# Decode with grouped attention and a gated feed-forward: the feed-forward's first two weight matrices are loaded at the start of the kernel instead of behind the last head's keys

## The chip, the cores and the metric

The kernel runs on one core of one Trainium2 chip. The metric is the device time of one execution in microseconds (us). The kernel before took 698.38 us, the median of three runs (697.04 to 698.63). Profiles, and all times of single instructions below, come from one profiled execution.

## The reference

One token `x` of width D = 512 goes through two branches, which a scalar gate mixes. All data are float32. Branch A is attention with 32 query heads over 8 key/value heads, 32768 cached positions and head size 128; the keys and values of one head are 16.8 MB each, 268 MB for all heads. Branch B is a SwiGLU feed-forward with F = 1792.

```python
g = sigmoid((x * gate_w).sum(-1))
q = (x @ wq).reshape(32, 128)                    # wq 512 x 4096
p = softmax(q . k_cache / sqrt(128))             # 4 query heads share a key head
a = (p . v_cache).reshape(4096) @ wo             # wo 4096 x 512
b = (silu(x @ w1) * (x @ w3)) @ w2               # w1, w3 512 x 1792, w2 1792 x 512
out = g * a + (1 - g) * b
```

## The kernel before, in words

**Three regions.** SBUF holds three tiles of 64 KB per partition, `ra`, `rb` and `rc` (L56). Each takes half of one head's keys or values, 8.39 MB. In the steady state `ra` holds the first half of a head's keys, `rb` the second half, and `rc` the first and then the second half of the values. So the values have only one region: the second half can't be loaded before the first is used up, nor the next head's first half before this head's second is.

**The load stream.** SP issues every large load (L112 to L146), each behind semaphore waits that say its region is free. At the start these are `wq` into `rc`, then the keys of head 0 into `ra` (two halves, L113 and L114) and `rb` (L115). Then, for each head h: the next head's first keys into `ra` once `scores(0)` of head h has read it (L120); the head's first values into `rc` once `values` of the previous head has read the second ones (L129, a wait for count 2h of `c_v`); the next head's second keys into `rb` once `scores(1)` has read it (L132); the second values into `rc` once the first are read (L134). For the last head there are no next keys. In their place L123 and L124 load `w1` and `w3` into `ra`, 3.67 MB each; the last second values go into `rb` (L136). Then `wo` goes into `ra`, behind a wait until the feed-forward's first products have read it (L138 to L140), and `w2` in four pieces into `rc` (L146).

```python
sp.wait_ge(c_v.sem, 2 * h)                                   # L126
sp.dma_start(rc, vd[h, 0]).then_inc(l_c, 16)                 # L129
sp.wait_ge(c_k.sem, 2 * h + 2)                               # L130
```

**The engines.** VectorE transposes each half of the keys in place in blocks of 32 x 32, eight instructions per half (`turned`, L290 to L295). TensorE's loop over heads (L273) has one body for all heads, with parts under an `If` that head 0 skips. Per head it does `scores(0)` on `ra`; the sum of the exponentials and `values(0)` of the previous head; `scores(1)` on `rb`; `values(1)` of the previous head; `flips`, which brings the scores of all positions of a query head together; `heads`; and `maxima`. VectorE then takes the maximum of the scores, and ScalarE computes the exponentials (L342) that the next iteration's `values` use. So the values of head h are used one iteration after its keys.

**The ends.** Ahead of the loop TensorE computes the gate's sum and the queries (L176, L182), and VectorE lays the queries out (L194, L198). Behind the loop come the gate and up rows of the feed-forward (`ff_rows`, L349 to L361: 16 products of 128 x 448 for each of `w1` and `w3`, two matmul records each), the sigmoid (L364), two multiplications (L366, L369) and a transpose into `htp` (L371); then the last head's `values`, and the products with `wo` and `w2` (L404 to L432). `htp`, `hid` and `omask` are cut out of the tile `sbuf` (L73 to L75), which the loop uses for the scores.

`take` (L105) is TensorE's wait for a token, which it counts down again. `c_k`, `c_v` and `c_e` are counts that `scores`, `values` and the products outside the loop raise when they end.

Of the kernel before, what the change touches and what calls it, by code (L numbers as in the profile page):

```python
# [4 lines left out]
AF = mybir.ActivationFunctionType  # L5
ALU = mybir.AluOpType
# [3 lines left out]
P = 128  # L10
# [14 lines left out]
@with_exitstack  # L25
def kernel(ctx, tc, x, k_cache, v_cache, wq, wo, w1, w3, w2, gate_w, out):
    with tc.tile_critical():
        _program(tc.nc, x, k_cache, v_cache, wq, wo, w1, w3, w2, gate_w, out)


def _program(nc, x, k_cache, v_cache, wq, wo, w1, w3, w2, gate_w, out):
    pe, dve, act, pool, sp = nc.tensor, nc.vector, nc.scalar, nc.gpsimd, nc.sync
    _, HKV, S, DH = k_cache.shape
    D = x.shape[-1]
    F = w1.shape[1]
    HQ = wq.shape[1] // DH
    REP = HQ // HKV
    NC = D // P
    FR = F // P
    FJ = F // 4  # L40
# [5 lines left out]
    def sb(name, *shape):  # L46
        return nc.alloc_sbuf_tensor(name, [P, *shape], F32).ap()

    def token(name):
        return nc.alloc_semaphore(name)  # L50

    def count(name):
        return Count(nc, name)


    ra, rb, rc = sb("ra", W), sb("rb", W), sb("rc", W)  # L56

    ident, ones, fold, dmask = sb("ident", P), sb("ones", P), sb("fold", 32), sb("dmask", 4)
    xs, gw, xp = sb("xs", NC), sb("gw", NC), sb("xp", NC, 32)
# [4 lines left out]
    ob = sb("ob", 512)  # L64
# [3 lines left out]
    gpr, gsm, gate = sb("gpr", NC), sb("gsm", 1), sb("gate", 2)  # L68
# [1 line left out]
    mr = nc.alloc_sbuf_tensor("mr", [REP, 1], F32).ap()  # L70
    md = nc.alloc_sbuf_tensor("md", [REP, REP], F32).ap()
    flat = sbuf.rearrange("p a i m -> p (a i m)")
    htp = flat[:, 0:FR * 32].rearrange("p (k i) -> p k i", i=32)  # L73
    hid = flat[:, 448:448 + FJ]
    omask = flat[:, 896:896 + P]  # L75

    qt = rc[:, 0:1024].rearrange("p (b q c i) -> p b q c i", b=2, q=4, c=4)

# [2 lines left out]
    def bank(n, w=1):  # L81
        return psum[:, 512 * n:512 * (n + w)]

    s_ps = [bank(0), bank(1)]
# [6 lines left out]
    l_w1, l_w3, l_v = token("l_w1"), token("l_w3"), token("l_v")  # L91
# [4 lines left out]
    c_q, c_k, c_v, c_f, c_m, c_n, c_h, c_e = (  # L96
        count(n) for n in ("c_q", "c_k", "c_v", "c_f", "c_m", "c_n", "c_h", "c_e")
    )
    c_dve, c_act, c_pool = count("c_dve"), count("c_act"), count("c_pool")

    t_x, t_tr, t_win, t_ev, t_ob, t_mx, t_md, t_p, t_e = (
        token(n) for n in ("t_x", "t_tr", "t_win", "t_ev", "t_ob", "t_mx", "t_md", "t_p", "t_e")
    )

    def take(sem, n=1):  # L105
        pe.wait_ge(sem, n).then_inc(sem, -n)  # L106
# [3 lines left out]
    vd = v_cache.rearrange("a h (r p n) d -> (a h) r p (n d)", r=2, p=P, n=NK)  # L110
    half = W // 2
    sp.dma_start(rc, wq.rearrange("(p c) n -> p (c n)", c=NC)).then_inc(l_q, 16)  # L112
    sp.dma_start(ra[:, 0:half], kd[0, 0][:, 0:half]).then_inc(l_k0, 16)  # L113
    l_a.by(sp.dma_start(ra[:, half:W], kd[0, 0][:, half:W]), 16)  # L114
    l_b.by(sp.dma_start(rb, kd[0, 1]), 16)  # L115
    for h in range(HKV):

        if h < HKV - 1:
            sp.wait_ge(c_k.sem, 2 * h + 1)
            l_a.by(sp.dma_start(ra, kd[h + 1, 0]), 16)  # L120
        else:
            sp.wait_ge(c_k.sem, 2 * h + 1)
            sp.dma_start(ra[:, 0:NC * F], w1.rearrange("(p c) f -> p (c f)", c=NC)).then_inc(l_w1, 16)  # L123
            sp.dma_start(ra[:, NC * F:2 * NC * F], w3.rearrange("(p c) f -> p (c f)", c=NC)).then_inc(l_w3, 16)  # L124
        if h:
            sp.wait_ge(c_v.sem, 2 * h)  # L126
        else:
            sp.wait_ge(c_dve.sem, 1)
        sp.dma_start(rc, vd[h, 0]).then_inc(l_c, 16)  # L129
        sp.wait_ge(c_k.sem, 2 * h + 2)  # L130
        if h < HKV - 1:
            l_b.by(sp.dma_start(rb, kd[h + 1, 1]), 16)  # L132
            sp.wait_ge(c_v.sem, 2 * h + 1)
            sp.dma_start(rc, vd[h, 1]).then_inc(l_c, 16)  # L134
        else:
            sp.dma_start(rb, vd[h, 1]).then_inc(l_v, 16)  # L136
    wod = wo.rearrange("(p k) e -> p (k e)", k=32)
    sp.wait_ge(c_e.sem, 2)  # L138
    for i in range(2):
        sp.dma_start(ra[:, i * half:(i + 1) * half], wod[:, i * half:(i + 1) * half]).then_inc(l_wo[i], 16)  # L140
    w2t = rc[:, 0:FR * D].rearrange("p (k e) -> p k e", e=D)
# [10 lines left out]
    local = count("local")  # L152
# [25 lines left out]
    for c in range(NC):  # L178
        for b in range(2):
            for j in range(4):  # L180
                o = (c * HKV + 4 * b + j) * REP * DH
                m = pe.matmul(  # L182
                    pq[b][32 * j:32 * j + 32, :], xp[:, c, :], rc[:, o:o + REP * DH],
                    start=(c == 0), stop=(c == NC - 1),
# [11 lines left out]
    for r in range(4):  # L196
        for j in range(4):
# [2 lines left out]
                qt[32 * j:32 * j + 32, :, :, :, 0].rearrange("p b q c -> p b c q"),  # L200
            )
    c_dve.by(m)


    for h in range(HKV):
# [12 lines left out]
    def scores(m, region):  # L218
        for f in range(2):
            for c in range(4):  # L220
                take(t_tr)
                for g in range(4):
                    n = 64 * f + 16 * g
                    w = 16 + 32 * c if f == 0 else 32 * c
                    i = pe.matmul(  # L225
                        s_ps[m][32 * g:32 * g + 32, :], winbuf[:, w:w + 32],
                        region.rearrange("p (n c i) -> p c n i", c=4, i=32)[:, c, n:n + 16],
                        start=(f == 0 and c == 0), stop=(f == 1 and c == 3),
                    )
        i.then_inc(c_k.sem, 1)  # L230

    def values(r, region):
        for g in range(4):
            for f in range(2):
                for t in range(4):
                    w = 512 * r + 64 * (2 * g + f) + 16 * t
                    n = 64 * f + 16 * g + 4 * t
                    i = pe.matmul(  # L238
                        o_ps[32 * t:32 * t + 32, :], prob[:, w:w + 32], region[:, n * DH:(n + 4) * DH],
                        start=(r == 0 and g == 0 and f == 0), stop=(r == 1 and g == 3 and f == 1),  # L240
                    )
        i.then_inc(c_v.sem, 1)

    def flips():
        take(t_ev, 2)
        for a in range(16):
            for s in range(2):
                i = pe.matmul(  # L248
                    pf[64 * s:64 * s + 64, 64 * a:64 * a + 64], sbuf[:, a].rearrange("p i m -> p (i m)"),
                    ident.rearrange("p (gf r s q) -> p s r gf q", gf=8, r=2, s=2)[:, s],  # L250
                    start=True, stop=True,
                )
        i.then_inc(c_f.sem, 1)

    def heads():
        take(t_ob)
        for b in range(4):
            i = pe.matmul(  # L258
                mb[:, 0:REP], ob[:, b * P:(b + 1) * P], fold[:, 4 * b:4 * b + 4], start=(b == 0), stop=(b == 3)
            )  # L260
        i.then_inc(c_h.sem, 1)

    def maxima():
        take(t_mx)
        pe.transpose(ma[0:REP, 0:P], mx, ident).then_inc(c_m.sem, 1)
        take(t_md)
        pe.matmul(ma[:, 128:128 + REP], ones[0:REP, :], md, start=True, stop=True).then_inc(c_m.sem, 1)

    def norm():
        take(t_p, REP)  # L270
        pe.matmul(mc[:, 0:REP], ones, sums, start=True, stop=True).then_inc(c_n.sem, 1)

    with nc.Fori(0, HKV, 1, engines=[PE]) as step:  # L273
        take(t_win, 4)
        scores(0, ra)
        with pe.If(step > 0):
            norm()
            take(l_c, 16)
            values(0, rc)
        scores(1, rb)  # L280
        with pe.If(step > 0):
            take(l_c, 16)
            values(1, rc)
        flips()
        with pe.If(step > 0):
            heads()
        maxima()
# [58 lines left out]
            ).then_inc(t_p, 1)  # L346


    def ff_rows(ps, base):  # L349
        for c in range(NC):  # L350
            for j in range(4):
                o = base + c * F + FJ * j
                i = pe.matmul(
                    ps[32 * j:32 * j + 32, 0:FJ], xp[:, c, :], ra[:, o:o + FJ], start=(c == 0), stop=(c == NC - 1)
                )
        i.then_inc(c_e.sem, 1)

    pe.wait_ge(l_w1, 16)
    ff_rows(s_ps[0], 0)
    pe.wait_ge(l_w3, 16)  # L360
    ff_rows(s_ps[1], NC * F)  # L361
    n_ff = 2
    act.wait_ge(c_e.sem, 1)
    n_sg = c_act.by(act.activation(ob[:, 0:FJ], s_ps[0][:, 0:FJ], AF.Sigmoid))  # L364
    dve.wait_ge(c_act.sem, n_sg)
    n_hid = local.by(dve.tensor_mul(hid, ob[:, 0:FJ], s_ps[0][:, 0:FJ]))  # L366
    dve.wait_ge(c_e.sem, 2)
    dve.wait_ge(local.sem, local.n)
    local.by(dve.scalar_tensor_tensor(hid, s_ps[1][:, 0:FJ], gate[:, 1:2], hid, op0=ALU.mult, op1=ALU.mult))  # L369
    dve.wait_ge(local.sem, local.n)  # L370
    dve.transpose(htp, hid.rearrange("p (a k) -> p k a", k=FR)).then_inc(t_e, 1)  # L371


    norm()
    pe.wait_ge(l_c, 16)
    values(0, rc)
    n_inv = inverted(HKV - 1)
    pe.wait_ge(l_v, 16)
    values(1, rb)
    act.wait_ge(local.sem, n_hid)  # L380
    act.wait_ge(c_v.sem, 2 * HKV)
    act.copy(ob, o_ps).then_inc(t_ob, 1)
    heads()
# [5 lines left out]
        otall.unsqueeze(2).to_broadcast([P, HQ, 4]),  # L389
        dmask.unsqueeze(1).to_broadcast([P, HQ, 4]),  # L390
    ).then_inc(t_e, 1)
    take(t_e, 2)
    pe.matmul(ma[:, 0:32], omask, fold, start=True, stop=True).then_inc(c_e.sem, 1)
    dve.wait_ge(c_e.sem, n_ff + 1)
    dve.tensor_copy(oq[:, 0:32], ma[:, 0:32]).then_inc(t_e, 1)
# [13 lines left out]
    for k in range(W2[1]):  # L409
        t = k % 4  # L410
        i = pe.matmul(  # L411
            acc[32 * t:32 * t + 32, :], htp[:, k, :], w2t[:, k, :], start=False, stop=(k >= W2[1] - 4),
            skip_group_check=True,
        )
# [52 lines left out]
```

## Time and profile before

| | |
|---|---|
| median of 3 runs | 698.38 us |
| profiled execution | 698.76 us |
| its span, first to last instruction | 696.7 us |
| moved from HBM | 296.23 MB, 425 GB/s over the span |
| busy TensorE / VectorE / ScalarE | 54% / 44% / 6% of the span |
| mean granted TensorE clock | 0.784 |

The rows that the sections below quote are of these kinds. A row of the timeline has the start in us from the span's start, the duration in us of one instruction or of a merged run of like ones, the engine and line, the operation, what it writes and reads, the count, and in brackets how long the engine had been idle and what ended that. `SPq` is SP's queue: the row of a load stands at its issue. A row of the list of DMA issues ends with the us from issue to landing, so that issue and this number give the landing. PE is TensorE, DVE VectorE, ACT ScalarE. "issue" as the cause of idle time means that nothing in the profile explains it.

### The profile page before, as it was taken

The numbers are of one execution on the slowest core, as the hardware profiler recorded it, in microseconds if no ns is written. First come the engines' busy times: TensorE is split into PE (matmuls) and PEld (weight loads), VectorE is DVE, ScalarE is ACT, GpSimd is POOL, SyncE is SP. The second block draws the span as 40 slices with busy tenths as digits, with TensorE's granted clock in tenths as the row PEclk, the third lists the DMA queues.
The fourth block names the chain that finished last, engine by engine and source line by source line (L and its number), as shares of the span: only waits on it lengthen the run. The fifth ranks groups of instructions, "written<-read, shape, count | busy, mean of one in ns | idle before, by whom it ended". The sixth has DMA issues, their size and how long they took to land. (4 is left out here: it accounts for less than half of the span.)

```text
span 696.7 us, 6587 instructions
## 1 busy us (share of the span) xinstructions
PE 374.5 (54%) x2944; PEld 104.0 (15%) x2944; DVE 307.9 (44%) x208; ACT 38.7 (6%) x94; POOL 7.1 (1%) x41
## 2 busy tenths in 40 slices
PE   0544457684727363664637472664638371781575
PEld 0100021030101210030101210030103110130122
DVE  0097573916345370917254470918163561810000
ACT  0000110001000100020000100020000100020000
POOL 0000000000000000000000000000000000000000
PEclk9987769787969787686859787687869686696689
DMA  9999998999999999999999999999999999999996
GB/s 399 412 453 411 430 419 369 421 425 467 433 421 421 421 478 425 421 421 433 463 429 421 421 433 463 429 421 421 433 463 429 422 421 433 426 459 426 425 419 276
DMA packets 6353, 296.35 MB, mean 425 GB/s; under 512 B 964, under 2 KB 968, under 8 KB 1224
## 3 DMA queue, kind: packets, MB, share of 16 engines
q1 hardware_dynamic: 6056, 296.23, 98.6%
q8 instruction: 6, 0.10, 0.1%
q10 hardware_dynamic: 288, 0.00, 0.0%
q14 instruction: 3, 0.02, 0.0%
HBM read 296.23 MB, written 0.00 MB: 425 GB/s over the span
## 5 line engine op out<-in xcount | busy, mean ns | idle before, releaser
L295 DVE STREAM_TRANSPOSE rb<-rb 128x2048 f32<-128x2048 f32 x64 | 141.8, 2275 | 141.5 <-DMA rb<-in_A_k_cache_dram 141.5
L225 PE MATMUL psum<-rb,winbuf 128*32 128x512 f32 x512 | 96.7, 835 | 133.6 <-PEq L106 133.5
L295 DVE STREAM_TRANSPOSE ra<-ra 128x2048 f32<-128x2048 f32 x64 | 141.3, 2274 | 39.6 <-DMA ra<-in_A_k_cache_dram 39.6
L225 PE MATMUL psum<-ra,winbuf 128*32 128x512 f32 x512 | 93.0, 801 | 106.0 <-PEq L106 106.0
L238 PE MATMUL psum<-rc,prob 128*32 128x512 f32 x960 | 114.8, 633 | 20.8 <-DMA rc<-in_A_v_cache_dram 16.5
L330 DVE TENSOR_REDUCE mx<-psum 128x4 f32<-128x1024 f32 x8 | 9.8, 1225 | 94.0 <-PE psum L248 94.0
L238 PEld LDWEIGHTS psum<-rc,prob 128*32 128x32 f32 x960 | 34.4, 116 | 96.5 <-issue 79.9
L225 PEld LDWEIGHTS psum<-rb,winbuf 128*32 128x32 f32 x512 | 13.6, 124 | 213.3 <-issue 213.3
L225 PEld LDWEIGHTS psum<-ra,winbuf 128*32 128x32 f32 x512 | 13.5, 122 | 177.3 <-issue 177.0
L310 ACT COPY sbuf<-psum 128x512 f32<-128x512 f32 x16 | 9.9, 620 | 469.0 <-PE psum L225 469.0
L299 DVE SCALAR_TENSOR_TENSOR otall<-psum,gate,recip 128x4 f32<-128x4 f32 x8 | 1.7, 214 | 45.1 <-PE psum L258 45.1
L248 PE MATMUL psum<-ident,sbuf 128*64 128x64 f32 x512 | 18.3, 233 | 5.7 <-issue 4.9
L342 ACT ACTIVATE prob<-psum,nm 128x256 f32<-128x256 f32 x32 | 18.9, 701 | 41.1 <-DVE nm L339 41.1
L248 PEld LDWEIGHTS psum<-ident,sbuf 128*64 128x64 f32 x512 | 17.0, 146 | 13.1 <-issue 13.1
L176 PE MATMUL psum<-gsm,ones 128*128 128x1 f32 x2 | 0.6, 348 | 26.1 <-PEq L106 26.1
L238 PE MATMUL psum<-rb,prob 128*32 128x512 f32 x64 | 8.7, 705 | 9.5 <-DMA rb<-in_A_v_cache_dram 9.5
L212 POOL COPY winbuf<-winraw 32x16 f32<-32x16 f32 x32 | 6.1, 191 | 523.2 <-PE psum L225 484.0
L404 PE MATMUL psum<-ra,oq 128*32 128x512 f32 x64 | 9.0, 711 | 4.2 <-DMA ra<-in_A_wo_dram 3.8
L169 DVE COPY xp<-xs 128x4 f32<-128x4 f32 x1 | 0.2, 171 | 23.2 <-DMA gw<-in_gate_w_dram 23.2
L258 PE MATMUL psum<-fold,ob 128*128 128x4 f32 x64 | 8.4, 255 | 0.9 <-PEq L106 0.9
L182 PE MATMUL psum<-rc,xp 128*32 128x512 f32 x64 | 8.6, 699 | 0.0
L258 PEld LDWEIGHTS psum<-fold,ob 128*128 128x128 f32 x64 | 7.7, 191 | 2.2 <-issue 1.7
(57 smaller groups left out, 71.3 us busy)
## 6 DMA issues: line engine op xcount, KB each, us to landing
ra<-in_A_k_cache_dram SPq DMA_DIRECT2D x2, 4096.0 KB, 36.0
ra<-in_A_wo_dram SPq DMA_DIRECT2D x2, 4096.0 KB, 50.7
ra<-in_B_w_dram SPq DMA_DIRECT2D x2, 3584.0 KB, 43.4
rc<-in_B_w_dram SPq DMA_DIRECT2D x1, 1536.0 KB, 32.7
rc<-in_B_w_dram SPq DMA_DIRECT2D x1, 1024.0 KB, 34.8
rc<-in_B_w_dram SPq DMA_DIRECT2D x1, 768.0 KB, 36.2
rc<-in_B_w_dram SPq DMA_DIRECT2D x1, 256.0 KB, 36.3
rc<-in_A_v_cache_dram SPq DMA_DIRECT2D x15, 31.4
```

What stands on the lines that cost most here:

```text
L182: m = pe.matmul(pq[b][32 * j:32 * j + 32, :], xp[:, c, :], rc[:, o:o + REP * DH], start=(c == 0), stop=(c == NC - 1),)
L212: pool.tensor_copy(winbuf[32 * r:32 * r + 32, 16:144].rearrange("p (c k) -> p c k", k=32)[:, :, 4 * r:4 * r + REP], winraw[32 * r:32 * r + ...
L225: i = pe.matmul(s_ps[m][32 * g:32 * g + 32, :], winbuf[:, w:w + 32], region.rearrange("p (n c i) -> p c n i", c=4, i=32)[:, c, n:n + 16], ...
L238: i = pe.matmul(o_ps[32 * t:32 * t + 32, :], prob[:, w:w + 32], region[:, n * DH:(n + 4) * DH], start=(r == 0 and g == 0 and f == 0), stop ...
L248: i = pe.matmul(pf[64 * s:64 * s + 64, 64 * a:64 * a + 64], sbuf[:, a].rearrange("p i m -> p (i m)"), ident.rearrange("p (gf r s q) -> p s ...
L258: i = pe.matmul(mb[:, 0:REP], ob[:, b * P:(b + 1) * P], fold[:, 4 * b:4 * b + 4], start=(b == 0), stop=(b == 3))
L295: dve.transpose(part[:, c], part[:, c]).then_inc(t_tr, 1)
L299: return local.by(dve.scalar_tensor_tensor(otall[:, REP * h:REP * h + REP], mb[:, 0:REP], gate[:, 0:1], recip, op0=ALU.mult, op1=ALU.mult))
L310: act.copy(sbuf[:, :, :, m], s_ps[m].rearrange("p (n i) -> p n i", i=32)).then_inc(t_ev, 1)
L330: dve.tensor_reduce(mx, pf.rearrange("p (a q) -> p q a", q=REP), axis=AX.X, op=ALU.max).then_inc(t_mx, 1)
L342: act.activation(prob[:, 0:1024].rearrange("p (a n q) -> p n a q", a=16, q=REP)[:, :, :, q], pf.rearrange("p (n a q) -> p n a q", n=16, q= ...
L404: pe.matmul(acc[32 * t:32 * t + 32, :], oq[:, k:k + 32], ra[:, k * D:(k + 1) * D], start=(k < 4), stop=False, skip_group_check=True,)
```

## The change

`w1` and `w3` go into `rb`, right behind `wq` in SP's order and ahead of all keys. The load of head 0's second keys into `rb` then has to wait until both products have read it. The gate and up rows, with all that follows up to `htp`, move from behind the loop to ahead of it. The loads in the last head's place are gone, and so is the wait ahead of `wo`. `htp` must now live through the loop, so it becomes a tile of its own (14 x 32 elements a partition); `hid` and `omask` move inside `sbuf`. TensorE takes the token of the finished `htp` ahead of the loop instead of behind it, and ScalarE's wait for `hid` ahead of its last copy goes.

```diff
-    htp = flat[:, 0:FR * 32].rearrange("p (k i) -> p k i", i=32)
-    hid = flat[:, 448:448 + FJ]
-    omask = flat[:, 896:896 + P]
+    omask = flat[:, 0:P]
+    hid = flat[:, P:P + FJ]
+    htp = sb("htp", FR, 32)
...
     sp.dma_start(rc, wq.rearrange("(p c) n -> p (c n)", c=NC)).then_inc(l_q, 16)
+    sp.dma_start(rb[:, 0:NC * F], w1.rearrange("(p c) f -> p (c f)", c=NC)).then_inc(l_w1, 16)
+    sp.dma_start(rb[:, NC * F:2 * NC * F], w3.rearrange("(p c) f -> p (c f)", c=NC)).then_inc(l_w3, 16)
     sp.dma_start(ra[:, 0:half], kd[0, 0][:, 0:half]).then_inc(l_k0, 16)
     l_a.by(sp.dma_start(ra[:, half:W], kd[0, 0][:, half:W]), 16)
+    sp.wait_ge(c_e.sem, 2)
     l_b.by(sp.dma_start(rb, kd[0, 1]), 16)
     for h in range(HKV):
 
         if h < HKV - 1:
             sp.wait_ge(c_k.sem, 2 * h + 1)
             l_a.by(sp.dma_start(ra, kd[h + 1, 0]), 16)
-        else:
-            sp.wait_ge(c_k.sem, 2 * h + 1)
-            sp.dma_start(ra[:, 0:NC * F], w1.rearrange("(p c) f -> p (c f)", c=NC)).then_inc(l_w1, 16)
-            sp.dma_start(ra[:, NC * F:2 * NC * F], w3.rearrange("(p c) f -> p (c f)", c=NC)).then_inc(l_w3, 16)
...
     wod = wo.rearrange("(p k) e -> p (k e)", k=32)
-    sp.wait_ge(c_e.sem, 2)
...
+    def ff_rows(ps, base):
...
+    pe.wait_ge(l_w1, 16)
+    ff_rows(s_ps[0], 0)
+    pe.wait_ge(l_w3, 16)
+    ff_rows(s_ps[1], NC * F)
...
+    dve.transpose(htp, hid.rearrange("p (a k) -> p k a", k=FR)).then_inc(t_e, 1)
...
+    take(t_e)
     with nc.Fori(0, HKV, 1, engines=[PE]) as step:
...
-    act.wait_ge(local.sem, n_hid)
     act.wait_ge(c_v.sem, 2 * HKV)
...
-    take(t_e, 2)
+    take(t_e)
```

The moved lines are those from L349 to L371, word for word but for `rb` in place of `ra` and `n_hid`, which is no longer kept.

More of the change, by code (lines that the diff above doesn't have):

```diff
@@ L202, in _program @@
     c_dve.by(m)
+    def ff_rows(ps, base):
+        for c in range(NC):
+            for j in range(4):
+                o = base + c * F + FJ * j
+                i = pe.matmul(
+                    ps[32 * j:32 * j + 32, 0:FJ], xp[:, c, :], rb[:, o:o + FJ], start=(c == 0), stop=(c == NC - 1)
+                )
+        i.then_inc(c_e.sem, 1)
+    pe.wait_ge(l_w1, 16)
+    ff_rows(s_ps[0], 0)
+    pe.wait_ge(l_w3, 16)
+    ff_rows(s_ps[1], NC * F)
+    n_ff = 2
+    act.wait_ge(c_e.sem, 1)
+    n_sg = c_act.by(act.activation(ob[:, 0:FJ], s_ps[0][:, 0:FJ], AF.Sigmoid))
+    dve.wait_ge(c_act.sem, n_sg)
+    local.by(dve.tensor_mul(hid, ob[:, 0:FJ], s_ps[0][:, 0:FJ]))
+    dve.wait_ge(c_e.sem, 2)
+    dve.wait_ge(local.sem, local.n)
+    local.by(dve.scalar_tensor_tensor(hid, s_ps[1][:, 0:FJ], gate[:, 1:2], hid, op0=ALU.mult, op1=ALU.mult))
+    dve.wait_ge(local.sem, local.n)
+    dve.transpose(htp, hid.rearrange("p (a k) -> p k a", k=FR)).then_inc(t_e, 1)
     for h in range(HKV):
@@ L346, in _program @@
             ).then_inc(t_p, 1)
[L349 to L371, printed above, removed]
     norm()
```

## The prediction
> **What bounds the kernel now.** I read the page's head first, then the DMA slices and queues, then the chain that ended last, and then the timeline where the change reaches.
>
> ```profile
> PE 374.5 (54%) x2944; PEld 104.0 (15%) x2944; DVE 307.9 (44%) x208; ACT 38.7 (6%) x94; POOL 7.1 (1%) x41
> DMA  9999998999999999999999999999999999999996
> GB/s 399 412 453 411 430 419 369 421 425 467 433 421 421 421 478 425 421 421 433 463 429 421 421 433 463 429 421 421 433 463 429 422 421 433 426 459 426 425 419 276
> q1 hardware_dynamic: 6056, 296.23, 98.6%
> ...
> 680.49 3.77 another core or an unknown queue
> ```
>
> No engine is over 54% busy, while SP's load queue is busy for 98.6% of the span, in every slice but the first heads and the end. Even the end waits for a load: the chain stands still for 3.77 us until the second half of `wo` is there. The kernel is one stream of loads. A change that moves the same bytes is worth only what it adds to or takes from the time in which that queue is **dry**. So the question is where the queue runs dry before and after, and I follow landings (issue plus time to landing).
>
> **The rate and the price of a dry queue.**
>
> ```profile
> 0.95 0.39 SPq L112 DMA_DIRECT2D rc<-in_A_wq_dram  x1
> 2.34 0.71 SPq L115 DMA_DIRECT2D rb<-in_A_k_cache_dram  x1
> 58.69 0.33 SPq L120 DMA_DIRECT2D ra<-in_A_k_cache_dram  x1
> 81.42 0.33 SPq L132 DMA_DIRECT2D rb<-in_A_k_cache_dram  x1
> 121.42 0.33 SPq L134 DMA_DIRECT2D rc<-in_A_v_cache_dram  x1
> ```
>
> Their times to landing, in the same order, from the list of DMA issues:
>
> ```profile
> rc<-in_A_wq_dram SPq DMA_DIRECT2D x1, 22.1
> rb<-in_A_k_cache_dram SPq DMA_DIRECT2D x1, 59.5
> ra<-in_A_k_cache_dram SPq DMA_DIRECT2D x1, 24.6
> rb<-in_A_k_cache_dram SPq DMA_DIRECT2D x1, 40.6
> rc<-in_A_v_cache_dram SPq DMA_DIRECT2D x1, 21.9
> ```
>
> `wq` lands at 23.05 and head 0's second keys at 61.84: 16.78 MB in 38.8 us, 432 GB/s, or 19.4 us for a region of 8.39 MB. Issued into an empty queue, the same bytes need 22.1 (`wq`) or 21.9 us (second values of head 0, issued 0.6 us ahead of the landing, at 122.0, of the keys before them). A dry queue thus costs the time between the landing before and the next issue, plus 21.9 - 19.4 = 2.5 us.
>
> **The end of the stream, where loads are removed.**
>
> ```profile
> 569.81 7.08 PE L238 MATMUL psum<-rc,prob 128*32 128x512 f32 x64
> 576.94 0.33 SPq L134 DMA_DIRECT2D rc<-in_A_v_cache_dram  x1
> 577.31 0.43 SPq L123 DMA_DIRECT2D ra<-in_B_w_dram  x1
> 588.89 8.89 DVE L295 STREAM_TRANSPOSE rb<-rb 128x2048 f32<-128x2048 f32 x4 [21.04 <-DMA rb<-in_A_k_cache_dram]
> 608.44 7.84 PE L238 MATMUL psum<-rc,prob 128*32 128x512 f32 x64
> 616.34 0.33 SPq L129 DMA_DIRECT2D rc<-in_A_v_cache_dram  x1
> 625.29 3.21 PE L353 MATMUL psum<-ra,xp 128*32 128x448 f32 x32 [1.09 <-DMA ra<-in_B_w_dram]
> 628.56 1.63 SPq L140 DMA_DIRECT2D ra<-in_A_wo_dram  x2
> 645.32 9.86 PE L238 MATMUL psum<-rc,prob 128*32 128x512 f32 x64 [16.51 <-DMA rc<-in_A_v_cache_dram]
> 664.68 8.72 PE L238 MATMUL psum<-rb,prob 128*32 128x512 f32 x64 [9.50 <-DMA rb<-in_A_v_cache_dram]
> ```
>
> The loads at 576.94 (the second values of head 6) and at 616.34 (the first of head 7) take, from issue to landing:
>
> ```profile
> rc<-in_A_v_cache_dram SPq DMA_DIRECT2D x1, 31.3
> ...
> rc<-in_A_v_cache_dram SPq DMA_DIRECT2D x1, 28.9
> ```
>
> The first lands at 608.24. The other, the next into `rc`, is issued only at 616.34, since `values(1)` (7.84 us from 608.44) must first have read `rc`, and that stands behind `scores(1)` in TensorE's order, which follows VectorE's eight transposes of the keys that landed at 588.89. Neither can move: the first four transposes alone take 8.89 us, and the other four as long. In between, the queue lives on `w1` and `w3`: they have landed by 625.29, 17.0 us after 608.24 (7.34 MB, 431 GB/s), so the issue at 616.34 comes 9 us before the queue would be empty. That is the cover which the change takes away; in the other heads it is the next head's first keys.
>
> After the change nothing stands in the queue behind the load that lands at 608.24. The first values of head 7, issued at 616.34 on this clock, land 21.9 us later, at 638.24. In the kernel before the landing is at 645.2, so the end comes 7.0 us earlier on this clock, for 17.0 us of bytes taken out. Everything up to there has moved back by the same 7.34 MB at the start, 17.0 us. **Sum: 17.0 - 7.0 = 10.0 us longer**; as a check, 616.34 - 608.24 + 2.5 gives 10.6 less 0.6 for this landing's cadence of 20.0 in place of 19.4. The price has ends: `values` on the rows of this kernel takes from 7.08 (at 569.81) over 7.84 to 9.86 us (at 645.32), so 9.2 to 12.0; I take 10.0, since the row with 7.84 is that very run of instructions.
>
> The rest of the end is neutral. `wo` loses its wait and is issued some 12 us sooner, but it was issued at 628.56, 36 us before the transfer ahead of it landed (664.68): nothing. `w2` still follows `values(0)` and is still queued behind `wo`. The feed-forward's 2 x 3.21 us of TensorE and its ScalarE and VectorE work lay inside the 16.51 us in which TensorE waited for head 7's values: freeing them gives nothing.
>
> **The start, where loads are added.**
>
> ```profile
> 25.54 0.17 DVE L169 COPY xp<-xs 128x4 f32<-128x4 f32 x1 [23.24 <-DMA gw<-in_gate_w_dram]
> 26.59 8.62 PE L182 MATMUL psum<-rc,xp 128*32 128x512 f32 x64
> 36.64 3.10 DVE L198 COPY winraw<-rc 32x32 f32<-32x32 f32 x16
> 39.76 17.66 DVE L295 STREAM_TRANSPOSE ra<-ra 128x2048 f32<-128x2048 f32 x8
> 625.03 0.55 ACT L364 ACTIVATE ob<-psum 128x448 f32<-128x448 f32 x1
> 625.61 0.62 DVE L366 TENSOR_TENSOR sbuf<-ob,psum 128x448 f32<-128x448 f32 x1 [4.35 <-ACT ob L364]
> 628.57 0.69 DVE L369 SCALAR_TENSOR_TENSOR sbuf<-psum,gate,sbuf 128x448 f32<-128x448 f32 x1 [2.34 <-PE psum L353]
> 629.29 0.94 DVE L371 STREAM_TRANSPOSE sbuf<-sbuf 128x448 f32<-128x448 f32 x1
> ```
>
> `wq` still lands at 23.05, `w1` then at 31.5, `w3` at 40.05, the two halves of head 0's first keys at 49.8 and 59.5. TensorE ends the queries at 35.2, does `w1`'s rows by 38.4 and `w3`'s from 40.1 to 43.3. ScalarE's 0.55 us and VectorE's 0.62 (behind its copies, which end at 39.74) lie in the wait for `w3`; then 0.69 + 0.94 end at 45.0, 4.8 us before the first keys land. So VectorE's transposes and TensorE's wait for `htp` don't delay anything; if this cover were gone, there are 10 more us until the second keys land, on which the next step hangs.
>
> **The added wait** is SP's for `c_e` at 2, met at 43.4. Behind it stand the load of head 0's second keys and all later loads. The queue still holds head 0's first keys until 59.5, a cover of 16 us. At nothing: head 0's second keys land at 59.5 + 19.4 = 78.9, which is 61.84 + 17.0. If the small load that holds up `xp` came only with `w1`, 6 us later, the first keys' cover of 4.8 us would be gone to within a microsecond, and the 10 us behind it would still hide that.
>
> **One gain and how it is lost.** Before, head 1's first keys are issued at 58.69, 3 us before the landing at 61.84, because VectorE started only at 39.76; they land at 83.3, 21.5 us after it instead of 19.4. After, VectorE starts at 49.8 and ends at 68.4, and the issue comes some 9 us ahead: up to 2.1 us back. But head 0's second values aren't bound by the stream. Their issue at 121.42 stands 59.6 us behind the landing at 61.84, through transposes, `flips`, maxima, exponentials, transposes and `values(0)`. That chain starts at the same landing and stays: issue at 138.5, landing at 160.4, against 143.3 + 17.0 = 160.3 before. So 0.0. It could only become shorter here:
>
> ```profile
> 82.17 0.65 PE L248 MATMUL psum<-ident,sbuf 128*64 128x64 f32 x14 [0.82 <-PEq L106]
> 87.68 3.04 PE L248 MATMUL psum<-ident,sbuf 128*64 128x64 f32 x50 [4.85 <-issue]
> ```
>
> In the first pass TensorE stops for 4.85 us within `flips`, waiting for nothing that the profile names. In the same 5 us the queue list has one transfer of instructions:
>
> ```profile
> q8 instruction: 1, 0.02, 1.1%
> ```
>
> I read it as a late fetch of code. The change puts 128 matmul and weight-load instructions ahead of this place, so the stop can move. If it goes, the chain loses 4.85 us, of which the stream uses at most 21.3 - 19.4 = 1.9 here plus the 2.1 above: -4.0. If a second one of its size falls into the chain, it costs +4.9. I take 0: the skipped parts of the body are the same.
>
> The Trainium skill, "Runtime: NRT & Kernel Launch", section "Instruction fetch mechanics", says that code is fetched in blocks of 16 KiB (256 instructions), ahead in sequence only, and that a taken branch to a block that isn't there stalls. By that page the stop stays, since head 0 still jumps over `values`, and the estimate would remain 0 with some tenths for the 14 products now behind it; no run here shows that yet.
>
> **Sum.** 698.76 + 10.0 + 0.0 = 708.8 us for an execution like the profiled one (span 696.7 and 2.1 around it). That one lies 0.4 above the median of the runs, so 708.4. The extreme terms, 9.2 - 4.0 and 12.0 + 4.9, seldom fall together.
>
> **The rivals.**
>
> 1. *The stop in `flips` goes* (above): 2 to 4 us less, 704.4 to 706.4. For it: nothing ties the stop to the work. Against it: the parts that head 0 skips ahead of it stay. 0.16.
> 2. *A second hold-up of the size of the stop enters the first head's chain*: 708.4 + 4.9 = 713.3. Against it: the covers of 4.8, 10 and 16 us. 0.08.
> 3. *The stream pays the dry time back*, and the time is the same or less. Place: the 28.8 MB from head 7's values on. Price: it needs 66.8 us at 432 GB/s; to win back 10 us it must run at 508 GB/s, and from there on the change is no loss; at 530 it would end 2.4 us faster, 696.0. For it: slices of up to 478 GB/s in the page's row, though beside slices of 421 to 425. Against it: after the dry queue at 121.42 the landing took 21.9 us, no less than `wq`'s 22.1. 0.03. The Trainium skill, "DMA: Bandwidth & Descriptors", section "Specifications", gives 435 GB/s as the fabric's ceiling; by it this rival can't be, and the 432 measured here lies just below.
>
> That the loads don't land in the new order can't be: they share one queue, and the waits are in the program.
>
> **How the numbers follow.** The forecast has the rest, 0.73. The range of 704.0 to 712.0 goes down to the lower end of `values` with all of rival 1's gain (708.4 - 0.8 - 4.0 = 703.6, a little within it), and up to the upper end of `values` with the 0.7 us of the 14 products (82.17 above) and the runs' own spread of 0.8 on either side (711.9). It leaves out rivals 2 and 3 and a few hundredths of tails, some 0.15. About 0.3% (2.1 us) is what a measurement can tell from no change; every case but rival 3 is beyond it. Rival 3 splits into 0.01 faster and 0.02 within: faster 0.01, same 0.02, slower 0.97.
>
> **What would show it.** In the profile after, the DMA slices have a dip shortly before head 7's first values, and the list of issues gives that load about 21.9 us to landing, not 28.9. Between its landing and the one before lie about 30 us instead of 19.4. SP's wait ahead of `wo` is gone, and the new one, ahead of head 0's second keys, ends near 43 with the queue full. Wrong would be a landing of head 7's first values less than 27 us after the one before, a first key landing delayed by the rows of the feed-forward, or a stream rate other than 432 GB/s for the early `w1` and `w3`.

## The result and the profile after

The changed kernel takes **706.23 us**, the median of 5 runs (705.89 to 707.14), beside 698.38 us for the kernel before (5 runs, 697.04 to 699.98): a ratio of 1.0112 with a 95% interval of 1.0095 to 1.0130, so 7.9 us slower. The forecast was 708.4, the range 704.0 to 712.0. The profiled execution took 706.43 us, with a span of 704.4, 7.7 above the 696.7 of before.

The page's head after, first the DMA slices and what they moved, then SP's load queue:

```profile
DMA  9999999999999999999999999999999999939996
GB/s 410 402 434 422 467 414 428 428 450 424 428 450 428 424 432 450 421 432 440 439 424 424 454 424 432 428 443 432 424 454 424 425 435 443 424 141 466 417 418 273
q1 hardware_dynamic: 6056, 296.23, 97.5%
```

The bytes are the same, 296.23 MB. One slice near the end stands out: the queue is busy 3 tenths and moves 141 GB/s. Before, no slice there was below 9. The stages around it, from the view by windows (the last two columns are the DMA share and GB/s; a packet counts where it starts, so both fall off ahead of a landing):

```profile
603.00:622.00 19.00, 10.70 (x64) 1.62 (x64) 17.73 (x9) 0.00 (x0) 0.00 (x0) 0.78 0.86 373
622.00:632.00 10.00, 9.48 (x134) 4.58 (x131) 0.13 (x1) 1.20 (x2) 0.00 (x0) 1.00 0.32 105
```

The timeline of that place, and then the times to landing of the loads at 591.16 and 629.86:

```profile
591.16 0.33 SPq L133 DMA_DIRECT2D rc<-in_A_v_cache_dram  x1
603.28 8.89 DVE L319 STREAM_TRANSPOSE rb<-rb 128x2048 f32<-128x2048 f32 x4 [21.05 <-DMA rb<-in_A_k_cache_dram]
622.74 7.07 PE L261 MATMUL psum<-rc,prob 128*32 128x512 f32 x64 [0.52 <-PEq L106]
629.86 0.33 SPq L128 DMA_DIRECT2D rc<-in_A_v_cache_dram  x1
652.89 8.54 PE L261 MATMUL psum<-rc,prob 128*32 128x512 f32 x64 [15.01 <-DMA rc<-in_A_v_cache_dram]
672.26 9.09 PE L261 MATMUL psum<-rb,prob 128*32 128x512 f32 x64 [10.84 <-DMA rb<-in_A_v_cache_dram]
...
692.00 3.64 PE L402 MATMUL psum<-ra,oq 128*32 128x512 f32 x32 [3.62 <-DMA ra<-in_A_wo_dram]
```

```profile
rc<-in_A_v_cache_dram SPq DMA_DIRECT2D x1, 31.4
...
rc<-in_A_v_cache_dram SPq DMA_DIRECT2D x1, 23.0
```

Head 6's second values land at 622.56. Nothing is queued behind them. `values` reads them until 629.8, then head 7's first values are issued, and they land at 652.86: 30.30 us behind the landing before, where a full queue has 19.4. This is the dry queue that the prediction worked out, in its place and order. The end still waits for `wo` (3.62 us), as before.

The start:

```profile
41.58 4.84 PE L207 MATMUL psum<-rb,xp 128*32 128x448 f32 x32 [2.80 <-DMA rb<-in_B_w_dram]
46.48 0.33 SPq L118 DMA_DIRECT2D rb<-in_A_k_cache_dram  x1
51.12 8.89 DVE L319 STREAM_TRANSPOSE ra<-ra 128x2048 f32<-128x2048 f32 x4 [2.97 <-DMA ra<-in_A_k_cache_dram]
80.20 17.66 DVE L319 STREAM_TRANSPOSE rb<-rb 128x2048 f32<-128x2048 f32 x8 [10.47 <-DMA rb<-in_A_k_cache_dram]
100.61 2.08 PE L271 MATMUL psum<-ident,sbuf 128*64 128x64 f32 x64 [0.82 <-PEq L106]
133.39 0.33 SPq L133 DMA_DIRECT2D rc<-in_A_v_cache_dram  x1
138.28 8.89 DVE L319 STREAM_TRANSPOSE rb<-rb 128x2048 f32<-128x2048 f32 x4 [15.08 <-DMA rb<-in_A_k_cache_dram]
```

The rows of the feed-forward do what was expected: SP's new wait ends at 46.48 instead of 43.4, still with the queue full until 60.8, and VectorE has done its share when it waits another 2.97 us for head 0's keys. Two things differ that matter. `w3` is there only at 41.57 instead of 40.05. And the first `flips` runs in one piece of 2.08 us: **the stop of 4.85 us is gone**. The records of `flips` are also quicker, 2.08 us for all 64 instead of 0.65 + 3.04, so the chain from the landing of head 0's second keys to the issue of its second values takes 53.2 us instead of 59.6. That issue now comes at 133.39, 4.9 us ahead of the landing of the keys before them instead of 0.6.

Landing by landing, after against before (us; a landing is issue plus time to landing, a distance is the time since the landing before):

| | before | after | shift |
|---|---|---|---|
| head 0's second keys | 61.84 | 80.18 | +18.34 |
| head 1's first keys, distance | 21.45 | 19.31 | -2.14 |
| head 0's second values, distance | 21.30 | 19.34 | -1.96 |
| all other loads up to head 6's second values | | | +0.1 |
| head 6's second to head 7's first values | 37.00 | 30.30 | -6.70 |
| from there to the end of the span | 51.46 | 51.54 | +0.08 |
| sum | | | +7.7 |

### The profile page after: what moved, and what is told of

It reads as the page before. It is cut to its first block, busy times and chain, and to the rows that moved or that the text cites. A ratio compares the mean times of both kernels' runs of the same rounds, so it can differ in the third digit from the quotient of the medians.

```text
span 704.4 us, 6586 instructions
## 1 busy us (share of the span) xinstructions
PE 364.7 (52%) x2944; PEld 101.5 (14%) x2944; DVE 308.1 (44%) x208; ACT 37.4 (5%) x93; POOL 7.1 (1%) x41
## 3 DMA queue, kind: packets, MB, share of 16 engines
q1 hardware_dynamic: 6056, 296.23, 97.5%
HBM read 296.23 MB, written 0.00 MB: 421 GB/s over the span
## 5 line engine op out<-in xcount | busy, mean ns | idle before, releaser
L248 PE MATMUL psum<-rb,winbuf 128*32 128x512 f32 x512 | 91.1, 790 | 148.1 <-PEq L106 148.1
L261 PE MATMUL psum<-rc,prob 128*32 128x512 f32 x960 | 111.4, 617 | 17.1 <-DMA rc<-in_A_v_cache_dram 15.0
L271 PE MATMUL psum<-ident,sbuf 128*64 128x64 f32 x512 | 16.7, 223 | 0.8 <-PEq L106 0.8
L207 PE MATMUL psum<-rb,xp 128*32 128x448 f32 x64 | 8.0, 653 | 2.8 <-DMA rb<-in_B_w_dram 2.8
L402 PE MATMUL psum<-ra,oq 128*32 128x512 f32 x64 | 7.3, 595 | 4.0 <-DMA ra<-in_A_wo_dram 3.6
```

Of the source, the lines that this page charges most:

```text
L207: i = pe.matmul(ps[32 * j:32 * j + 32, 0:FJ], xp[:, c, :], rb[:, o:o + FJ], start=(c == 0), stop=(c == NC - 1))
L248: i = pe.matmul(s_ps[m][32 * g:32 * g + 32, :], winbuf[:, w:w + 32], region.rearrange("p (n c i) -> p c n i", c=4, i=32)[:, c, n:n + 16], ...
L261: i = pe.matmul(o_ps[32 * t:32 * t + 32, :], prob[:, w:w + 32], region[:, n * DH:(n + 4) * DH], start=(r == 0 and g == 0 and f == 0), stop ...
L271: i = pe.matmul(pf[64 * s:64 * s + 64, 64 * a:64 * a + 64], sbuf[:, a].rearrange("p i m -> p (i m)"), ident.rearrange("p (gf r s q) -> p s ...
L402: pe.matmul(acc[32 * t:32 * t + 32, :], oq[:, k:k + 32], ra[:, k * D:(k + 1) * D], start=(k < 4), stop=False, skip_group_check=True,)
```

## The experiments

The theory behind all of them: the load stream is the clock, and the change moves the time only by where the stream runs dry. The rivals: the end is bound by the work behind the last values, or the moved work delays the first head. A second question was why the stop went and what it was.

**1. Head 7's first values into another region.** This takes the wait away by giving it nothing to wait for.

```diff
+            sp.wait_ge(c_k.sem, 2 * h + 1)
+            sp.dma_start(ra, vd[h, 0]).then_inc(l_v0, 16)      # h = 7
...
+    sp.wait_ge(c_v.sem, 2 * HKV - 2)                            # wo now into rc, w2 into ra
+        sp.dma_start(rc[:, i * half:(i + 1) * half], ...).then_inc(l_wo[i], 16)
...
-    values(0, rc)
+    values(0, ra)
```

> The changed kernel, but head 7's first values go into ra (free once scores(0) of head 7 has read the keys), wo into rc and w2 into ra. Theory: the 7.7 us net loss is the load queue running dry ahead of head 7's first values (30.3 us from the landing before to theirs, where a full queue has 19.4). With another region for them their load is issued some 30 us sooner, the landing distance goes to 19.4, and the time falls by 10.9 to about 695.5 us, 2.9 below the kernel before. Rival: the wait is not what costs, the end is held by the products behind the last values, or the stream pays dry time back: then the distance goes to 19.4 as well, but the time stays above 703.

Measured: 695.35 us (6 runs), ratio to the kernel before 0.9959 (0.9945 to 0.9974).

```profile
592.03 0.43 SPq L126 DMA_DIRECT2D ra<-in_A_v_cache_dram  x1
642.31 8.50 PE L266 MATMUL psum<-ra,prob 128*32 128x512 f32 x64 [3.24 <-DMA ra<-in_A_v_cache_dram]
661.66 9.06 PE L266 MATMUL psum<-rb,prob 128*32 128x512 f32 x64 [10.85 <-DMA rb<-in_A_v_cache_dram]
```

The load is issued 31 us ahead of the landing at 622.96 and lands 19.3 us behind it. The span is 693.5, 10.9 below the changed kernel's 704.4: the whole dry time comes back, to a tenth. The theory holds, the rivals fall. This version is faster than both kernels, by 0.4% beside the kernel before.

**2 and 3. The code ahead of the loop made longer.** The same 32 small products, once in the kernel before, once in the changed one.

```diff
+    for b in range(2):
+        for c in range(NC):
+            for j in range(4):
+                pe.matmul(s_ps[b][32 * j:32 * j + 32, 0:P], xp[:, c, :], ones, start=(c == 0), stop=(c == NC - 1))
```

> The kernel before, with 32 small products of xp and ones (128 columns, results never read) put into TensorE's program right behind the queries, as many instructions as the rows of the feed-forward. Nothing else. Theory: the stop of 4.85 us in the first flips is a fetch of code at a block boundary, and only moving the code made it go. Then the first flips runs in one piece (2.1 us instead of 0.65 + 4.85 + 3.04), head 0's second values are issued near 116.5 instead of 121.4 and land 19.4 us behind the keys before them instead of 21.3: about 696.5 us. Rival: the stop belongs to what the loads or the clock do at that moment: it stays, and the time is 698.4.

Measured: 696.85 us (12 runs), ratio 0.9976 (0.9963 to 0.9989). The first `flips`, the issue of head 0's second values, and its time to landing:

```profile
83.35 2.08 PE L254 MATMUL psum<-ident,sbuf 128*64 128x64 f32 x64 [0.82 <-PEq L106]
116.11 0.33 SPq L134 DMA_DIRECT2D rc<-in_A_v_cache_dram  x1
...
rc<-in_A_v_cache_dram SPq DMA_DIRECT2D x1, 25.5
```

Products whose results nobody reads made the kernel before 1.5 us faster. The stop is gone, and the values land at 141.61, 19.3 us behind the keys before them instead of 21.3.

> The changed kernel with the same 32 small products ahead of the loop, so that the code of the loop stands about 256 instructions further on than in the kernel before. Theory of code blocks of 256 instructions: the stop in the first flips is back at nearly the place of the kernel before (after some 12 to 14 of its products), head 0's second values are issued near 138.3 and land about 21.3 us behind the keys before them instead of 19.3: 706.2 + 2.0 = 708.2 us. Rival: the stop came from the loads or from timing: it stays away, 706.2.

Measured: 708.78 us (4 runs), ratio to before 1.0145 (1.0130 to 1.0161), 2.6 us above the changed kernel.

```profile
100.57 0.98 PE L271 MATMUL psum<-ident,sbuf 128*64 128x64 f32 x13 [0.81 <-PEq L106]
104.99 3.04 PE L271 MATMUL psum<-ident,sbuf 128*64 128x64 f32 x51 [3.45 <-issue]
140.27 0.33 SPq L133 DMA_DIRECT2D rc<-in_A_v_cache_dram  x1
```

The stop is back, after 13 records of `flips` where the kernel before had 14. In this execution head 0's second values were issued not near 138.3 but 2.0 us behind the landing of the keys before them, and landed 23.8 us behind it instead of the expected 21.3. It took 710.91, the longest of the four; the other three took 708.6 to 708.9.

**4. The changed kernel without the moved work.** The feed-forward's part of the output is left out.

```diff
-    sp.wait_ge(c_e.sem, 2)
+    sp.wait_ge(l_w1, 16)
+    sp.wait_ge(l_w3, 16)
     l_b.by(sp.dma_start(rb, kd[0, 1]), 16)
...
-    pe.wait_ge(l_w1, 16)
-    ff_rows(s_ps[0], 0)
...
+    dve.memset(htp, 0.0).then_inc(t_e, 1)
```

> The changed kernel without the gate and up rows and what follows from them (htp is set to zero, so the feed-forward's part of the output is left out); w1 and w3 are still loaded, and the load of head 0's second keys waits for their landing alone. Theory: the moved work costs nothing where it stands, so the landings of head 0's keys stay as in the changed kernel; its code is again as long as before ahead of the loop, so the stop in flips is back and costs 2.0 us: 708.2. If w3's slow landing (10.1 us behind w1 instead of 8.6) came from TensorE reading w1 out of rb in that time, w3 is 1.4 us quicker here: 706.8. Rival, that the moved work delays the first head: the keys of head 0 land or are used sooner by a us or more, and the time is below 706.

Measured: 709.49 us (4 runs, 708.47 to 710.91), ratio 1.0163 (1.0144 to 1.0182). Without the work the kernel is no faster than the changed one; it is slower (708.2 was expected), since the stop is back:

```profile
100.44 0.59 PE L251 MATMUL psum<-ident,sbuf 128*64 128x64 f32 x13 [0.82 <-PEq L106]
104.84 3.04 PE L251 MATMUL psum<-ident,sbuf 128*64 128x64 f32 x51 [3.81 <-issue]
137.81 0.33 SPq L134 DMA_DIRECT2D rc<-in_A_v_cache_dram  x1
```

So the moved work costs nothing, and head 0's second keys land at 80.10, as in the changed kernel (80.18). `w3` is quick here, 8.6 us behind `w1` instead of 10.1. But it isn't TensorE's reading of `rb` that had held it: the 1.3 us turn up later instead, since head 0's second keys need 20.66 us. What moved along is the first packet of code (a transfer of instructions, in queue q8). `w3`'s time to landing (issued at 1.87 in both) and that packet, in the stretch from 39 to 40 us of the changed kernel:

```profile
rb<-in_B_w_dram SPq DMA_DIRECT2D x1, 3584.0 KB, 39.7
...
q8 instruction: 1, 0.02, 6.2%
```

The same without the moved work, the packet in the stretch from 73 to 74:

```profile
rb<-in_B_w_dram SPq DMA_DIRECT2D x1, 3584.0 KB, 38.2
...
q8 instruction: 1, 0.02, 6.8%
```

The last column is the share of 16 engines, so one packet takes one engine for 1.0 us (6.2% of 16 in 1 us). In the changed kernel it falls into `w3`; here into those keys; in the padded kernel of experiment 2 at 38.0, within the second half of head 0's first keys, which need 11.0 us there instead of 9.7.

**5. Where the 2.1 us of head 1's first keys came from.** In the changed kernel, SP also waits for some copies on ScalarE before it issues these keys: eight, ten, and nine.

```diff
+            if h == 0:
+                sp.wait_ge(late.sem, 8)
             l_a.by(sp.dma_start(ra, kd[h + 1, 0]), 16)
...
+            if h == 0 and m == 0:
+                for i in range(8):
+                    act.wait_ge(late.sem, i)
+                    late.by(act.copy(ob, s_ps[0]))
```

> The changed kernel, but head 1's first keys are issued later: SP also waits for eight copies on ScalarE (nothing reads them), so that the issue comes about 3 us ahead of the landing of head 0's second keys, as in the kernel before, instead of 9.2 us. Theory now: the 2.1 us that head 1's first keys lost in the kernel before (21.5 us behind the landing before instead of 19.4) did not come from the late issue, but from the first fetch of code, one packet of 16 KB that occupies one DMA engine for 1.0 us at 60 to 61 us; in the changed kernel the same loss sits in w3 (10.1 instead of 8.6, packet at 39 to 40). So here the distance stays 19.3 and the time 706.2. Rival, as the prediction had it: a lead of 3 us is too short, the distance is 21.4 again, and with head 0's second values issued 5 us ahead of their turn the whole loss reaches the end: 708.3.

Measured: 706.89 us (5 runs, 706.24 to 709.49, two of them above 709), ratio to before 1.0138 (1.0117 to 1.0160); the span of the profiled execution is that of the changed kernel, 704.4. The issue came 3.9 us ahead of the landing before (its lead), not 3.15 as in the kernel before, so this did not yet test the case.

> As the kernel with eight copies, which had its issue 3.9 us ahead of the landing and lost nothing, but with ten, so the issue of head 1's first keys comes about 2.7 us ahead. Seen so far: leads of 3.9 us and more lose nothing, 3.3 to 3.5 lose 0 to 0.9, and 2.5, 0.6 and 0.4 lose about 2. Theory: a lead below about 3.2 us costs a nearly fixed 2 us, so the 2.1 us of the kernel before (lead 3.15) were the late issue, as the prediction had it: the distance is 21.3 here, 708.3 us. Rival, the code packet alone: the distance stays 19.4, 706.3 us. A loss in proportion (21.9 less the lead, where that is over 19.4) would also leave 19.4.

> The same with nine copies, a lead of about 3.3 us, beside the 3.15 of the kernel before. Theory of the late issue: on the edge, a distance between 19.4 and 21.4, 706.3 to 708.3 us. Rival: 19.4, 706.3 us.

Measured: ten copies 707.97 us (4 runs), ratio 1.0137 (1.0111 to 1.0164); nine copies 707.44 us (2 runs), ratio 1.0130 (1.0096 to 1.0165). The issue and the time to landing with eight copies, and then with ten:

```profile
76.25 0.33 SPq L125 DMA_DIRECT2D ra<-in_A_k_cache_dram  x1
...
ra<-in_A_k_cache_dram SPq DMA_DIRECT2D x1, 23.3
```

```profile
78.24 0.33 SPq L125 DMA_DIRECT2D ra<-in_A_k_cache_dram  x1
...
ra<-in_A_k_cache_dram SPq DMA_DIRECT2D x1, 22.9
```

The keys before them land at 80.15 and 79.97. With a lead of 3.9 us the distance is 19.40, with 1.7 us it is 21.17, and the next load takes some tenths more. With nine copies (lead 2.2) the two loads together lose 1.4. The loads are the same and the first packet of code stands at 38 to 39 us in all three, so **the late issue is enough for such a loss**. Whether the kernel before lost its 2.1 us at a lead of 3.15 us to the lead alone stays open, since a packet of code stands there too, at 60 to 61 us, and a lead of 2.2 cost less than that. The kernel of experiment 2 has a packet at the same place, and there the same two loads lose 1.2 us together with a lead of 4.3; so the packet may have had a part in the 2.1.

**6. Other bytes as the cover.** Half of `wo` goes ahead of head 7's first values.

```diff
+        else:
+            sp.wait_ge(c_k.sem, 2 * h + 1)
+            sp.dma_start(ra[:, 0:half], wod[:, 0:half]).then_inc(l_wo[0], 16)
...
-    for i in range(2):
+    for i in range(1, 2):
```

> The changed kernel, but the first half of wo (4.19 MB) is loaded into ra ahead of head 7's first values, as cover in the place of the removed w1 and w3. Theory: that half lands 9.7 us behind head 6's second values, 2 to 3 us after the issue of head 7's first values, so the queue is not dry, and the last values land about 1.2 us sooner than in the changed kernel (30.3 us become 9.7 + 19.4). But the work behind the last values, which the two halves of wo covered, is now the bound: 12.5 us to the first product with wo, 7.3 for both halves, and some 9 to the end: about 701 us, up to 704 at a low clock. Rival: the end is bound by the loads alone, so all the 10.9 us come back: 695.5.

Measured: 702.92 us (4 runs, 701.71 to 704.98; the profiled one is the longest), ratio to before 1.0061 (1.0044 to 1.0077).

```profile
630.00 0.33 SPq L132 DMA_DIRECT2D rc<-in_A_v_cache_dram  x1
653.87 8.79 PE L264 MATMUL psum<-rc,prob 128*32 128x512 f32 x64 [15.86 <-DMA rc<-in_A_v_cache_dram]
673.23 9.35 PE L264 MATMUL psum<-rb,prob 128*32 128x512 f32 x64 [10.57 <-DMA rb<-in_A_v_cache_dram]
686.19 9.69 PE L405 MATMUL psum<-ra,oq 128*32 128x512 f32 x64 [0.38 <-PEq L106]
```

The bound has changed: the 64 records with `wo` run in one piece from 686.19 with no wait for a load, and the chain that ended last, which the profile follows back to 686.15 and no further, holds nothing but TensorE and the last copy. In the changed kernel the same place waits 3.62 us for the second half of `wo`. In one point the expectation was off: the half lands at 632.48, 2.5 us after the issue of the values, and that lead again cost 2.0 (distance 21.32), so the last values landed no sooner.

**7. More code beside the stream.** The kernel of experiment 1 with TensorE's loop written out.

```diff
-    with nc.Fori(0, HKV, 1, engines=[PE]) as step:
+    for step in range(HKV):
...
-        with pe.If(step > 0):
+        if step:
```

> The kernel with head 7's values in ra, with TensorE's loop over heads written out eight times (the parts under If left out for head 0), so that its code is some 19 blocks of 16 KB longer and every one is fetched beside the load stream. Theory that a code packet costs the stream only where the engine that carries it has no slack: each takes one of 16 engines for 1.0 us, and if always the same one has to carry them, up to 19 us are lost (714); if they are spread evenly, 19 / 16 = 1.2 us (696.6). Rival: code packets cost the stream nothing, the loss in w3 has another cause: 695.4 or, with the stalls behind branches gone, a little less.

Measured: 699.09 us (10 runs), ratio to before 1.0003 (0.9990 to 1.0016), 3.7 us above experiment 1.

```profile
q8 instruction: 23, 0.38, 0.2%
```

There are 23 packets of code instead of 6. None of the three numbers was right. The landings lose in steps, of 0.9 and 1.1 us at head 0's second values and head 2's first keys, then 1.1 and 1.0 at two later loads and some tenths at two more; all other distances are 19.3 to 19.4. The first of these steps has a lead of 3.5 us and no packet of code in flight, so the lead may be its cause; each of the others has one or two packets in flight, while most packets cost nothing. So code takes time from the stream, far less than a packet's 1.0 us each time. That the engine with the least slack decides, and the packets are spread unevenly, fits this, but no view tells which DMA engine carried which packet; it stays an argument.

## Why the prediction was right, and where it failed

**What bounds the kernel**: right. The sum of the distances of landings gives the 7.7 us of the span, and experiment 1 gives back the dry time alone.

**The end of the stream**, 17.0 - 7.0 = 10.0: right in mechanism and nearly in size. The distance is 30.30 us where 30.0 was forecast. Two deviations cancel: `values` took 7.07 us instead of 7.84, and the load into the empty queue took 23.0 instead of 21.9. Within the kernel before, the same distance was 37.0, so the end gives 6.7 where 7.0 was forecast.

**The early loads**, 17.0: mis-sized. Head 0's second keys came 18.34 us later. The 1.3 us are the first packet of code, which now falls into `w3` (experiment 4). Among its signs of being wrong the prediction had a rate other than 432 GB/s for the early `w1` and `w3`, and this one came: `w3`'s 3.67 MB took 10.07 us, 364 GB/s.

**The moved work and the new wait** at nothing: right, shown by experiment 4 and by the queue, which was full until 60.8 when the wait ended at 46.48. (The "14 products" that the range allows for are 14 records, two to a product.)

**One gain and how it is lost**: half right, and the step that failed. The gain at head 1's first keys came, 2.14 us, and a short lead can cost nearly that much (experiment 5); how much of it was the lead and how much a packet of code that stood there and now falls into `w3` stays open. But it wasn't lost again. The step said of the stop in `flips`: "I take 0: the skipped parts of the body are the same". The skipped parts are the same, and the stop went all the same, since it hangs on where the code stands. With that chain 6.4 us shorter, head 0's second values are issued early enough, and both losses are gone: -4.1, where rival 1 had "-4.0" as its limit. The measured 706.23 lies within rival 1's 704.4 to 706.4; I gave it 0.16. So it was a rival that came true, and the range holds because it took that rival in; that the time came only 2.2 below the forecast is in part luck, since the packet in `w3`, which the sum didn't have, took back 1.3 of the 4.1.

The Trainium skill, "Runtime: NRT & Kernel Launch", section "Instruction fetch mechanics", has code in blocks of 256 instructions. The runs agree: 128 instructions more ahead of the loop take the stop away (experiment 2 and the change itself), 256 bring it back to within one record of its place (experiment 3), and taking 128 away again does too (experiment 4). The same section says that a taken branch to a block that isn't there stalls; I used it to keep the stop. In the changed kernel head 0 takes the same branches over `values`, and no row of TensorE shows a stall behind them; whether the block was there, no view shows.

**Rival 2**, a second hold-up, and **rival 3**, dry time paid back, did not come: after the dry queue the distances are 19.37 and 9.68 for half a region, as anywhere. The sum of the errors: +1.3 for the packet of code, -4.1 for the stop and the lead, +0.3 at the end and +0.2 of small shifts, together -2.3; the profiled execution missed the 708.8 of the sum by 2.4.

## What to carry to other kernels

In a kernel that is one stream of loads, ask of each load that you move what stood behind it in the queue: here `w1` and `w3` were the only thing that kept the queue busy while a region was being read, and earlier bytes buy nothing where every byte is paid for anyway. Before you look for other bytes as a cover, look for another region for the load that waits: that gave all 10.9 us, where half of `wo` ahead of it gave 3.3 and left the end bound by the products behind the last values. And before a difference of some microseconds is put down to an edit, look whether a stop with no cause in the profile has come or gone with the place of the code.

## What the runs showed of the hardware

- **A load issued 2.5 us or less ahead of the landing before it lost some 2 us.** Leads of 0.4, 0.6, 1.7 and 2.5 us each lost about 2 us (experiment 4, the kernel before, experiments 5 and 6) and one of 2.2 lost 1.4; those of 3.3 to 3.5 us lost between 0 and 0.9 (experiments 1, 6 and 7). Leads of 3.9 and 4.9 lost nothing (distances 19.40 and 19.34), while with a packet of code in flight one of 3.15 lost 2.1 (the kernel before) and one of 4.3 lost 1.2 over two loads (experiment 2). So the loss looks like a nearly fixed 2 us, not the lead that is missing. In the changed kernel the last packet ahead of the dry stretch starts before 620, and that load lands at 622.6; that this lag is the reason is not shown.
- **A packet of code slows the load stream.** It is 16 KB and takes one DMA engine 1.0 us. In all the kernels with a packet at 37 to 40 us it cost the first loads 1.0 to 1.5 us; the next two cost mostly nothing, but 1.2 at 60.7 us in experiment 2. The kernel with 17 packets more took 3.7 us longer.
- **Work that does nothing can make a kernel faster**: 32 products more, 1.5 us less (0.9963 to 0.9989).
